# The first DFT stage of batch 1 on quarters of the array: two half-loads, four tied matmuls, two stores a step

## The chip, the core and the metric

The kernel runs on one core of a Trainium2 chip. The metric is the device time of one execution in microseconds (us); several executions are timed and the median counts. One further execution was recorded by the hardware profiler, and all rows shown here come from that one.

## What is computed

The program chains three layers. The change lies in the first, which transforms a tensor of 4 batches, 3072 positions and 256 channels along the positions, applies a complex weight matrix with soft thresholding to the spectrum, and transforms back:

```python
X = np.fft.rfft(x, axis=1)
Yr = Xr @ w_r - Xi @ w_i + b_r
Yi = Xr @ w_i + Xi @ w_r + b_i
Yr, Yi = soft_threshold(Yr, 0.01), soft_threshold(Yi, 0.01)
y = np.fft.irfft(Yr + 1j * Yi, n=3072, axis=1)
```

The second layer sends each token to one of 8 experts (up to 384 tokens each, in order of position), and the third is a feed-forward layer with a gate. Since the experts fill up early, batch 0 and the first third of batch 1 are usually all that is needed; batches 2 and 3 stand in a branch (`far`) that is not taken with these inputs.

## The kernel before

The transform of 3072 points is split into 48 times 64. For batch 1 the **first stage** is `s1`: a 48-point transform over positions that lie 64 apart. Its input is laid out as 96 rows (48 positions, times 2 interleaved halves of the 64), and its table `c1` is a 96 x 96 matrix that holds the 48 x 48 table twice, spread by an identity of size 2, so half of its entries are zero. `s1` walks over 8 pieces of 1024 columns. For each piece, SyncE's queue (SP) loads `xt` (96 rows of 4 KB), TensorE (PE) makes two float32 matmuls of 96 x 96 by 512 columns into one PSUM bank each (pool `ps`, 3 banks), ScalarE (ACT) or VectorE (DVE) copies each bank to `ao`, and SP stores `ao` to `a_d` in DRAM. The profile calls the two `ps<-xt,c`, L406, and a float32 matmul shows as two records, since it is made in two passes.

Around it runs the **spectral stage of batch 0**, `kphase`, in steps over pairs of frequencies: four transposes into `at` (L430, from the same pool `ps`), four float32 matmuls into `xp` (L438), 24 short matmuls into `yp` (L207 to L209), two float32 matmuls into `bp` (L489); ACT and DVE cut and threshold in between, and ACT stores `b_d`. A third stream, `ffn_in`, fetches and reshapes weights of the last layer (`nt`, 512 KB each, and `mixed`). A fourth loads the tables `c2` and `c3` piece by piece (`c<-in_tab`, `c<-in_inv`). `mix` draws steps from these generators in proportion to given lengths, and a scheduler then sets each engine's instruction order when the program is built; on the chip each engine's order is fixed, and so is the order of DMAs on SP's queue.

`self.after(ins, first)` asks only that one instruction stands behind another in that order. After this stretch comes `is2`, the inverse stage of batch 0, which already works on quarters of the array through `tiled` (L363): 48 rows of input on partitions 0 to 47, 48 on 64 to 111, and outputs on PSUM partitions 0 to 63 and 64 to 127.

Of the kernel before, what the change touches and what calls it, by code (L numbers as in the profile page):

```python
# [9 lines left out]
F32 = mybir.dt.float32  # L10
# [6 lines left out]
B, S, D = 4, 3072, 256  # L17
N1, N2 = 48, 64
NK = 24
Q = 96  # L20
TW = 32
E, F, CAP = 8, 1024, 384
DFF = 2048
P = 128
# [25 lines left out]
def _tables():  # L50

    n = float(S)
    t1 = np.arange(N1)
    t2 = np.arange(N2)
    c1 = np.zeros((N1, NK, 2))  # L60
    c4 = np.zeros((NK, 2, N1))
    alt = np.where(t1 % 2 == 0, 1.0, -1.0)
    c1[:, 0, 0] = 1.0
    c1[:, 0, 1] = alt
    c4[0, 0] = 1.0 / n
    c4[0, 1] = alt / n
    for k in range(1, NK):
        a = 2 * np.pi * ((k * t1) % N1) / N1
        c1[:, k, 0] = np.cos(a)
        c1[:, k, 1] = -np.sin(a)  # L70
        c4[k, 0] = 2 * np.cos(a) / n
        c4[k, 1] = -2 * np.sin(a) / n
    eye2 = np.eye(2)
    c1 = np.einsum("akr,pz->apkrz", c1, eye2).reshape(Q, Q)
    third = np.einsum("kra,pz->krpaz", c4[:, :, :QB // 2], np.eye(2)).reshape(Q, QB)

    def halves(t):
        t = np.pad(t.reshape(N1, N1), ((0, 64 - N1), (0, 64 - N1)))
        return np.concatenate([t, t])

    c4 = np.concatenate([halves(c4), np.pad(third, ((0, P - Q), (0, 0)))], axis=1)
    m = np.zeros((NK, 2, N2, 2, N2))
    s = np.arange(N2)
    for k in range(1, NK):
        f = k + N1 * s
        a = 2 * np.pi * ((t2[:, None] * f[None]) % S) / S
        sg = np.where(f > S // 2, -1.0, 1.0)[None]
        co, si = np.cos(a), np.sin(a)
        m[k, 0, :, 0], m[k, 1, :, 0] = co, si
        m[k, 0, :, 1], m[k, 1, :, 1] = -si * sg, co * sg  # L90
    alt2 = np.where(t2 % 2 == 0, 1.0, -1.0)
    inv0 = np.zeros((2, N2, 2, N2))
    for half, f0 in ((0, 0), (1, N1 // 2)):
        for j in range(32):
            f = f0 + N1 * j
            if f == 0:
                continue
            a = 2 * np.pi * ((t2 * f) % S) / S
            sl = 32 * half + j
            m[0, half, :, 0, sl] = np.cos(a)  # L100
            m[0, half, :, 1, sl] = -np.sin(a)
            inv0[0, sl, half] = 2 * np.cos(a)
            inv0[1, sl, half] = -2 * np.sin(a)
    prime = np.concatenate([-m[0, :, :, 1], m[0, :, :, 0]], axis=2).reshape(P, P)
    m[0, 0, :, 0, 0] = 1.0
    m[0, 0, :, 1, 0] = alt2
    inv0[0, 0, 0] = 1.0
    inv0[1, 0, 0] = alt2
    m = m.reshape(NK, P, P)
    tab = np.concatenate([prime, m[0], m[1:].transpose(1, 0, 2).reshape(P, -1)], axis=1)  # L110
    inv = np.concatenate([inv0.reshape(P, P), m[1:].transpose(2, 0, 1).reshape(P, -1)], axis=1)
    ind = np.zeros((2, 2, P))
    ind[:, 0, :64] = 1.0
    ind[:, 1, 64:] = 1.0
    ind[0, 0, 64] = 1.0
    ind[0, 1, 64] = 0.0
    ind = ind.transpose(1, 0, 2).reshape(2, 2 * P)
    u, q = np.arange(P) // QB, np.arange(P) % QB
    at = TW * q + GT * u
    tri = (at[:, None] < at[None]).astype(np.float32)  # L120
    tok = 1 + at[:, None] + (TW * QB * np.arange(3)[:, None] + np.arange(GT)).reshape(1, -1)
    out = {
        "c1": c1,
        "c4": c4,
        "tab": tab,
        "inv": inv,
        "ind": ind,
        "rt": np.concatenate([tri, np.ones((P, P)), tok], axis=1),
    }
    return {k: np.ascontiguousarray(v, np.float32) for k, v in out.items()}  # L130
# [24 lines left out]
class Kernel:  # L155
    def __init__(self, ctx, tc, i, o):
        self.tc, self.nc, self.i, self.o = tc, tc.nc, i, o
        nc = self.nc
        cst = ctx.enter_context(tc.tile_pool(name="cst", bufs=1))
        self.dr = ctx.enter_context(tc.tile_pool(name="dr", bufs=1, space=bass.MemoryType.DRAM))  # L160
        self.zt = cst.tile([P, 1, D], F32, name="zt")
        nc.vector.memset(self.zt, 0.0)
        self.ident = cst.tile([P, P], F32, name="ident")
        make_identity(nc, self.ident)
        self.table = cst.tile([P, NF, SC * E], F32, name="table")
        self.carry = cst.tile([P, E], F32, name="carry")
        nc.gpsimd.memset(self.carry, 0.0)
        nc.gpsimd.memset(self.table, 0.0)
        self.attn = [self.dr.tile([n, D], F32, name=f"attn{h}") for h, n in enumerate((NEAR, NT - NEAR))]
        self.cst = cst  # L170
        self.tail = cst.tile([P, SC, 2, D], F32, name="tail")
        self.mixed = self.dr.tile([DFF // D, P, 3, P], F32, name="mixed")
        self.zeroed = 0
        self.stored, self.fetched, self.spread = {}, None, None
        self.again, self.away, self.evicted, self.gated = False, False, None, {}
        self.held, self.lasty = {}, None

# [41 lines left out]
    @contextmanager  # L219
    def consts(self, tag):  # L220

        with self.tc.tile_pool(name=f"bc{tag}", bufs=2, side="right") as bc:
            self.bc = bc
            self.c1 = bc.tile([Q, Q], F32, name="c1", bufs=1)
            self.nc.sync.dma_start(out=self.c1, in_=self.i["c1"])
            yield

    @contextmanager
# [23 lines left out]
    def near(self):  # L252

        ads, self.bds, self.res = {}, {}, {}
        self.left = ExitStack()
        self.kp = self.left.enter_context(self.tc.tile_pool(name="kpa", bufs=2, reuse_waits="tile"))
        with self.stream("a", 3, "right"), self.sums("a", 2):
            self.warm()
            self.first()
            tables, spectra = self.load_tables(), self.kphase(0, ads)  # L260
            for g in (tables, spectra, tables, spectra, spectra):
                next(g)
            mix([tables, spectra, self.s1(1, ads), self.ffn_in(0, 6, 0)], [4, 10, 24, 7], lead=[0, 0, 0, 0])
            rest = self.kphase(1, ads, True)
            next(rest)
            with self.tc.issue_after(self.fetched):
                self.route_consts()
            mix([self.is2(0, (0, 1, 2), self.res), self.ffn_in(6, 8, 5)], [10, 7])
            self.route(0, (0, 1, 2), self.res)
            self.rank()  # L270
            self.early = self.slots(self.cst, 0, EARLY, self.sel, "s")[0]
            for _ in rest:
                pass
# [80 lines left out]
    CH = 512  # L354
    LD = 1024

    def tiled(self, table, rows, pool):

        out = [pool.tile([P, self.CH], F32, tag="ps", name="ps1") for _ in range(2)]
        for ch in range(2):  # L360
            for p in range(2):
                at = slice(64 * p, 64 * p + N1)
                self.nc.tensor.matmul(out[p][64 * ch:64 * ch + 64], table[at, :64], rows[at, ch * self.CH:(ch + 1) * self.CH],  # L363
                                      start=True, stop=True)
        return out

    def first(self):
# [23 lines left out]

    def s1(self, b, ads):
        nc, bp, ps, CH, LD = self.nc, self.bp, self.ps, self.CH, self.LD
        xv = self.i["x"].rearrange("b (q t) c -> b q (t c)", t=TW)
        a_d = ads[b] = self.dr.tile([NK, P, D], F32, name=f"a_d{b}")
        av = a_d.rearrange("k (r t) c -> (k r) (t c)", r=4)
        for n in range(TW * D // CH):
            half = slice(n * CH % LD, n * CH % LD + CH)
            if half.start == 0:
                ld = slice(n * CH, n * CH + LD)  # L400
                xt = bp.tile([Q, LD], F32, tag="xt", name="xt", bufs=self.sb)
                ao = bp.tile([Q, LD], F32, tag="ao", name="ao1", bufs=self.sb)
                ins = nc.sync.dma_start(out=xt, in_=xv[b, :, ld])
                self.after(ins.ins, self.fetched)
            pt = ps.tile([Q, CH], F32, tag="ps", name="ps1")
            nc.tensor.matmul(pt, self.c1, xt[:, half], start=True, stop=True)  # L406
            self.hi("aava"[n % 4], ao[:, half], pt)
            if half.stop == LD:
                self.stored.setdefault(b, []).append(nc.sync.dma_start(out=av[:, ld], in_=ao).ins)
            yield  # L410

    def kphase(self, b, ads, ahead=False):
# [938 lines left out]
```

## Time and profile before

| | us |
|---|---|
| median of 3 runs (616.84 to 617.54) | 617.31 |
| the profiled execution | 615.97 |
| its span, first to last instruction | 614.2 |
| PE busy in the span | 593.2 (97%) |
| DVE busy | 420.4 (68%) |
| ACT busy | 338.7 (55%) |
| GpSimd (POOL) busy | 196.8 (32%) |

The profiled execution lies 1.3 us under the median of the timed runs, and 1.8 us of it lie outside the span. The mean granted clock of TensorE is 0.993 of its full 2.4 GHz. 86.09 MB were moved by DMA. An engine's busy time is that of its records; PE's records overlap, so the distance from one start to the next tells what a matmul costs, and not its length.

### The profile page before, as it was taken

To read this page: it belongs to the slowest core of one execution; us is meant where nothing else is said; L and a number is where in the kernel's file an instruction comes from. 1 tells how busy PE (TensorE), PEld (TensorE's weight loads), DVE (VectorE), ACT (ScalarE), POOL (GpSimd) and SP (SyncE) were. 2 spreads that over 40 slices of the span, in tenths; PEclk is the share of its full clock that TensorE was granted. 3 is DMA by queue.
4 is the path that set the end of the run, shared out by engine and by line. 5 is a ranking of instruction groups with operands and counts; after the bars stand their busy time and mean duration, and the time that the engine had idled before them with its cause. 6 is when DMAs were issued, how large, how long until landed. Compare 5 with 4: busy or idle time off the path is not lost. (4 is left out here: it accounts for less than half of the span.)

```text
span 614.2 us, 11459 instructions
## 1 busy us (share of the span) xinstructions
PE 593.2 (97%) x4116; PEld 553.2 (90%) x4116; DVE 420.4 (68%) x838; ACT 338.7 (55%) x722; POOL 196.8 (32%) x195
## 2 busy tenths in 40 slices
PE   9999999998999799989999999999999999999993
PEld 9887899666988578979999999999999999999993
DVE  2477775358977579999876785586587677476562
ACT  2646554345535464567755666665567556375561
POOL 1001010001056243267563505435403442163433
PEclk9999999999999999999999999999999999999998
DMA  8838775984456989211734543404533230010001
GB/s 225 253 94 272 251 227 166 246 268 123 162 179 208 259 272 295 92 52 44 222 118 133 154 125 103 153 17 138 153 106 112 85 105 22 5 66 27 16 2 56
DMA packets 65755, 86.09 MB, mean 140 GB/s; under 512 B 5812, under 2 KB 55608, under 8 KB 65688
## 3 DMA queue, kind: packets, MB, share of 16 engines
q1 hardware_dynamic: 53720, 69.53, 37.7%
q10 hardware_dynamic: 9664, 9.44, 5.2%
q0 software_dynamic: 2304, 6.29, 3.2%
q8 instruction: 34, 0.56, 0.4%
q14 instruction: 33, 0.27, 0.1%
HBM read 54.31 MB, written 30.93 MB: 139 GB/s over the span
## 5 line engine op out<-in xcount | busy, mean ns | idle before, releaser
L1249 DVE TENSOR_TENSOR u<-h,u 128x384 f32<-128x384 f32 x224 | 117.8, 552 | 57.2 <-PE h L209 48.3
L1172 ACT ACTIVATE u<-u 128x384 f32<-128x384 f32 x128 | 64.1, 522 | 69.4 <-DVE u L1249 68.8
L208 PE MATMUL o<-wo,gl 128*128 128x256 f32 x366 | 97.9, 280 | 1.5 <-DVE gl L199 1.5
L209 PE MATMUL o<-wo,gh 128*128 128x256 f32 x366 | 98.0, 280 | 0.0
L207 PE MATMUL o<-wo,gh 128*128 128x256 f32 x366 | 86.2, 280 | 0.1
L199 POOL TENSOR_TENSOR ring<-mt,ring 128x384 fp32r<-128x384 f32 x32 | 38.3, 1199 | 128.6 <-ACT ring L191 117.7
L199 POOL TENSOR_TENSOR gl<-u,gh 128x384 fp32r<-128x384 f32 x62 | 65.2, 1068 | 31.6 <-ACT gh L191 27.2
L208 PEld LDWEIGHTS o<-wo,gl 128*128 128x128 f32 x366 | 68.8, 188 | 1.8 <-DVE gl L199 1.8
L209 PEld LDWEIGHTS o<-wo,gh 128*128 128x128 f32 x366 | 68.8, 188 | 0.0
L191 ACT CAST gh<-u 128x384 fp32r<-128x384 f32 x126 | 63.3, 510 | 4.8 <-PE o L209 3.1
L207 PEld LDWEIGHTS o<-wo,gh 128*128 128x128 f32 x366 | 64.4, 188 | 0.4 <-ACT gh L191 0.4
L207 PE MATMUL yp<-wri,xk 128*128 128x256 f32 x188 | 56.2, 299 | 0.0
L1094 DVE SCALAR_TENSOR_TENSOR hl<-hp,hh 128x384 fp32r<-128x384 f32 x64 | 35.2, 552 | 28.6 <-ACT hh L1093 24.8
L209 PE MATMUL yp<-wri,xk 128*128 128x256 f32 x188 | 54.0, 287 | 0.0
L208 PE MATMUL yp<-wri,xk 128*128 128x256 f32 x188 | 53.6, 285 | 0.2 <-issue 0.2
L191 ACT CAST w<-st 128x512 fp32r<-128x512 f32 x64 | 38.7, 619 | 25.2 <-DMA st<-in_moe_w 17.6
L1093 ACT ACTIVATE hh<-hp 128x384 fp32r<-128x384 f32 x64 | 31.0, 490 | 36.7 <-PE y L208 17.3
L199 DVE TENSOR_TENSOR w<-st,w 128x512 fp32r<-128x512 f32 x53 | 38.4, 734 | 18.5 <-ACT w L191 14.0
L199 POOL TENSOR_TENSOR wi<-na,wi 128x256 fp32r<-128x256 f32 (+1 forms) x8 | 8.1, 1011 | 127.7 <-ACT wi L191 127.7
L207 PE MATMUL y<-hh,w 128*128 128x384 f32 x128 | 43.5, 341 | 1.8 <-ACT w L191 1.8
L207 PE MATMUL hp<-xT,w 128*128 128x384 f32 x128 | 43.4, 340 | 1.4 <-ACT w L191 0.7
L208 PE MATMUL y<-hh,w 128*128 128x384 f32 x128 | 43.3, 338 | 0.0
(248 smaller groups left out, 1529.2 us busy)
## 6 DMA issues: line engine op xcount, KB each, us to landing
st<-in_moe_w SPq DMA_DIRECT2D x64, 256.0 KB, 3.0
out<-zt SPq DMA_DIRECT2D x48, 256.0 KB, 2.9
b_d<-bo ACTq DMA_DIRECT2D x12, 512.0 KB, 3.0
mt<-mixed SPq DMA_DIRECT2D x32, 192.0 KB, 2.4
xt<-in_x SPq DMA_DIRECT2D x15, 384.0 KB, 6.3
nt<-in_moe_w_in SPq DMA_DIRECT2D x8, 512.0 KB
nt<-in_moe_w_out SPq DMA_DIRECT2D x16, 256.0 KB, 8.1
a_d<-ao SPq DMA_DIRECT2D x8, 384.0 KB, 3.0
```

The costliest lines, as they stand in the source:

```text
L191: self.lastact = self.nc.scalar.copy(dst, src)
L199: return e.tensor_tensor(dst, src, raw(hi), ALU.subtract).ins
L207: first = nc.tensor.matmul(out, lh, rh, start=start, stop=False)
L208: nc.tensor.matmul(out, ll, rh, start=False, stop=False)
L209: return first.ins, nc.tensor.matmul(out, lh, rl, start=False, stop=stop).ins
L1093: self.rectified = nc.scalar.activation(hh, hp, AF.Relu).ins
L1094: self.evicted = nc.vector.scalar_tensor_tensor(hl, hp, 0.0, raw(hh), ALU.max, ALU.subtract).ins
L1172: act.activation(sg, sg, AF.Silu)
L1249: v.tensor_tensor(to, h, u, ALU.add)
```

## The change

The 48-point table is now also kept in its small form, padded to 64 x 64 on both partition halves (`c1h`), beside the old one, which the first stage of batch 0 still uses; the constant load grows from 96 x 96 to 128 x 160 values. In `s1` a piece's input comes as two loads of 48 rows, to partitions 0 to 47 and 64 to 111. The two matmuls of 96 x 96 by 512 become four of 48 x 64 by 512 by way of `tiled`, in the order upper rows, lower rows, upper, lower, each set behind the one before it by `after`. Each of the two banks now holds 128 x 512 and is copied as before (three of four by ACT). The result leaves in two stores of 48 partitions with rows of 2 KB, in place of one with rows of 4 KB. `s1` has 8 steps where it had 16, and its length in `mix` goes from 24 to 12.

```diff
+    small = c1.copy()
     c1 = np.einsum("akr,pz->apkrz", c1, eye2).reshape(Q, Q)
...
+    wide = np.pad(c1, ((0, P - Q), (0, 0)))
+    c1 = np.concatenate([wide, halves(small)], axis=1)
...
-            self.c1 = bc.tile([Q, Q], F32, name="c1", bufs=1)
-            self.nc.sync.dma_start(out=self.c1, in_=self.i["c1"])
+            c1 = bc.tile([P, Q + 64], F32, name="c1", bufs=1)
+            self.nc.sync.dma_start(out=c1, in_=self.i["c1"])
+            self.c1, self.c1h = c1[:Q, :Q], c1[:, Q:]
...
-            mix([tables, spectra, self.s1(1, ads), self.ffn_in(0, 6, 0)], [4, 10, 24, 7], lead=[0, 0, 0, 0])
+            mix([tables, spectra, self.s1(1, ads), self.ffn_in(0, 6, 0)], [4, 10, 12, 7], lead=[0, 0, 0, 0])
...
-    def tiled(self, table, rows, pool):
+    def tiled(self, table, rows, pool, order=(0, 1)):
 
         out = [pool.tile([P, self.CH], F32, tag="ps", name="ps1") for _ in range(2)]
+        ins = None
         for ch in range(2):
-            for p in range(2):
+            for p in order:
                 at = slice(64 * p, 64 * p + N1)
-                self.nc.tensor.matmul(out[p][64 * ch:64 * ch + 64], table[at, :64], rows[at, ch * self.CH:(ch + 1) * self.CH],
-                                      start=True, stop=True)
+                prev, ins = ins, self.nc.tensor.matmul(out[p][64 * ch:64 * ch + 64], table[at, :64], rows[at, ch * self.CH:(ch + 1) * self.CH],
+                                                       start=True, stop=True).ins
+                if prev and order[0]:
+                    self.after(ins, prev)
...
-        xv = self.i["x"].rearrange("b (q t) c -> b q (t c)", t=TW)
+        xv = self.i["x"].rearrange("b (a p t) c -> b p a (t c)", p=2, t=TW)
         a_d = ads[b] = self.dr.tile([NK, P, D], F32, name=f"a_d{b}")
-        av = a_d.rearrange("k (r t) c -> (k r) (t c)", r=4)
-        for n in range(TW * D // CH):
...
+        av = a_d.rearrange("k (r z t) c -> (k r) z (t c)", r=2, z=2)
+        for n in range(TW * D // LD):
+            xt = bp.tile([P, LD], F32, tag="xt", name="xt", bufs=self.sb)
+            ao = bp.tile([P, 2, CH], F32, tag="ao", name="ao1", bufs=self.sb)
+            for p in range(2):
+                ins = nc.sync.dma_start(out=xt[64 * p:64 * p + N1], in_=xv[b, p, :, n * LD:(n + 1) * LD])
                 self.after(ins.ins, self.fetched)
...
+            for p, pt in enumerate(self.tiled(self.c1h, xt, ps, (1, 0))):
+                self.hi("aava"[2 * n % 4 + p], ao[:, p], pt)
+            for ch in range(2):
+                nc.sync.dma_start(out=av[:, :, n * LD + ch * CH:][:, :, :CH], in_=ao[64 * ch:64 * ch + N1])
             yield
```

The instruction order of PE, ACT, DVE and SP differs between the two programs only from the first matmul of `s1` (37.54 us in the profile before) to about 84 us, apart from the branch that is not taken, the constant load at the start, and the first loads of `xt` that are now pairs. From there on the four engines have the same rows in the same order. Three places follow.

The first place is PE's order where `s1` begins, right behind the first `bp` pair; `ps` is a PSUM bank, `c_78` the table `c1`. Before:

```order
L489 MATMUL bp<-cl,c_226 128x256 x2
L406 MATMUL ps_432<-xt,c_78 96x512
L406 MATMUL ps_446<-xt,c_78 96x512
L438 MATMUL xp<-c_225,ar 128x128 x4
L207 MATMUL yp<-wri,xk 128x256
L208 MATMUL yp<-wri,xk 128x256
L406 MATMUL ps_453<-xt,c_78 96x512
```

The same place of the changed program, where `tiled` is L368:

```order
L493 MATMUL bp<-cl,c_226 128x256 x2
L368 MATMUL ps_434<-xt,c_78 64x512
L368 MATMUL ps_433<-xt,c_78 64x512
L368 MATMUL ps_434<-xt,c_78 64x512
L368 MATMUL ps_433<-xt,c_78 64x512
L442 MATMUL xp<-c_225,ar 128x128 x4
L368 MATMUL ps_459<-xt,c_78 64x512
```

Step 0 stands in one piece, and behind `xp` comes a single matmul of step 1. Sixteen short matmuls into `yp` follow it, and then the rest of step 1:

```order
L210 MATMUL yp<-wri,xk 128x256
L368 MATMUL ps_458<-xt,c_78 64x512
L368 MATMUL ps_459<-xt,c_78 64x512
L368 MATMUL ps_458<-xt,c_78 64x512
L434 MATMUL at<-ident,xs 128x128 x4
```

Step 1 is cut in 1 and 3. Steps 2 to 5 stand in one piece each; the first matmul of step 7 stands right behind the four of step 6, and the other three come ten `yp` matmuls later. So 9 pieces of quarter matmuls stand between other work, where before the 16 matmuls of full size stood.

The second place is SP's queue, from the store of step 0 on (`a_d`; the table pieces are `in_tab` and `in_inv`). Before:

```order
L409 DMA a_d_428<-ao_430 96x1024
L307 DMA c_225<-in_tab 128x768
L307 DMA c_226<-in_inv 128x768
L403 DMA xt<-in_x 96x1024
L409 DMA a_d_428<-ao_451 96x1024
L871 DMA nt<-in_moe_w_in 128x1024
L919 DMA mixed<-mt 128x2x384
L403 DMA xt<-in_x 96x1024
```

In the changed program, from the same store to the second load of `xt` behind it:

```order
L413 DMA a_d_428<-ao_430 96x1x512 x2
L413 DMA a_d_428<-ao_455 96x1x512 x2
L311 DMA c_225<-in_tab 128x768
L311 DMA c_226<-in_inv 128x768
L408 DMA xt<-in_x 48x1024 x2
L875 DMA nt<-in_moe_w_in 128x1024
L413 DMA a_d_428<-ao_539 96x1x512 x2
L923 DMA mixed<-mt 128x2x384
L408 DMA xt<-in_x 48x1024 x2
```

The two tables, and with them step 3's load, stood behind the store of step 0 and stand now behind the store of step 1 (`ao_455`) as well; the store of step 2 (`ao_539`) stands now ahead of step 4's load, the last row of both pieces.

## Rows read from the trace of the kernel before

**Rows 1.** The page: PE's busy time, and PE's busy tenths in 40 slices of 15.4 us.

```profile
PE 593.2 (97%) x4116; PEld 553.2 (90%) x4116; DVE 420.4 (68%) x838; ACT 338.7 (55%) x722; POOL 196.8 (32%) x195
...
PE   9999999998999799989999999999999999999993
```

**Rows 2.** Windows from 37 us: length, busy us (records) by engine, PEclk, DMA share, GB/s.

```profile
37.00:60.00 23.00, 23.00 (x141) 18.08 (x140) 18.01 (x32) 13.50 (x28) 3.48 (x4) 1.00 0.74 227
60.00:82.00 22.00, 22.00 (x140) 17.58 (x138) 16.24 (x28) 13.13 (x28) 3.60 (x4) 1.00 0.81 265
82.00:110.00 28.00, 28.00 (x219) 27.09 (x218) 17.03 (x30) 12.95 (x29) 1.28 (x1) 1.00 0.61 183
110.00:135.00 25.00, 25.00 (x203) 15.47 (x202) 10.03 (x26) 10.26 (x20) 0.00 (x0) 1.00 1.03 269
```

**Rows 3.** Timeline of PE where `s1` begins: start us, us, engine, line, operation, tiles, shapes.

```profile
36.68 1.03 PE L489 MATMUL bp<-cl,c 128*128 128x256 f32 x4
37.54 1.88 PE L406 MATMUL ps<-xt,c 96*96 96x512 f32 x4
39.26 1.06 PE L438 MATMUL xp<-c,ar 128*128 128x128 f32 x8
40.07 0.36 PE L207 MATMUL yp<-wri,xk 128*128 128x256 f32 x1
40.27 0.28 PE L208 MATMUL yp<-wri,xk 128*128 128x256 f32 x1
...
41.97 0.60 PE L430 MATMUL at<-ident,xs 128*128 128x128 f32 x4
42.32 0.36 PE L209 MATMUL yp<-wri,xk 128*128 128x256 f32 x1
42.52 0.28 PE L207 MATMUL yp<-wri,xk 128*128 128x256 f32 x1
42.64 0.28 PE L208 MATMUL yp<-wri,xk 128*128 128x256 f32 x1
```

**Rows 4.** Timeline of PE in `is2`, which works on quarters (L363).

```profile
110.60 1.08 PE L363 MATMUL ps<-br,c 48*64 48x512 f32 x4
111.61 1.13 PE L489 MATMUL bp<-cl,c 128*128 128x256 f32 x4
112.67 1.09 PE L363 MATMUL ps<-br,c 48*64 48x512 f32 x8
113.69 0.39 PE L207 MATMUL yp<-wri,xk 128*128 128x256 f32 x1
113.91 0.28 PE L208 MATMUL yp<-wri,xk 128*128 128x256 f32 x1
```

**Rows 5.** Lines of ACT and DVE, 37 to 85 us: PSUM copies; busy us, mean ns.

```profile
L191 ACT COPY ao<-ps 96x512 f32<-96x512 f32 x12 | 6.9, 583 | 3.8 <-PE ps L406 1.8 <-DMA xt<-in_x 1.1 <-ACT bo L191 0.5
...
L193 DVE COPY ao<-ps 96x512 f32<-96x512 f32 x4 | 2.7, 680 | 0.4 <-PE ps L406 0.4
```

**Rows 6.** Timeline of SP's queue: issue time, issue us; store, table, step 3's, step 4's load.

```profile
40.28 0.33 SPq L409 DMA_DIRECT2D a_d<-ao  x1
40.66 0.42 SPq L307 DMA_DIRECT2D c<-in_tab  x1
...
41.94 0.45 SPq L403 DMA_DIRECT2D xt<-in_x  x1
...
51.16 0.42 SPq L403 DMA_DIRECT2D xt<-in_x  x1
```

**Rows 7.** Window 41 to 55 us; last columns PEclk, DMA share, GB/s.

```profile
41.00:55.00 14.00, 14.00 (x86) 10.88 (x86) 11.16 (x20) 7.98 (x17) 2.74 (x3) 1.00 0.92 282
```

**Rows 8.** Source view of the loads of `xt` in `s1` (L403).

```profile
DMA to landing us min/median/max: 5.5/6.3/7.6
```

**Rows 9.** Windows around the one fall of TensorE's granted clock; columns as in group 2.

```profile
205.00:212.80 7.80, 5.32 (x27) 4.21 (x26) 2.78 (x6) 3.29 (x7) 1.97 (x2) 1.00 1.08 274
212.80:216.20 3.40, 3.40 (x13) 1.30 (x14) 3.37 (x6) 1.63 (x3) 1.84 (x2) 0.50 1.07 258
```

More of the change, by code (lines that the diff above doesn't have):

```diff
@@ L173, in __init__ @@
         self.zeroed = 0
-        self.stored, self.fetched, self.spread = {}, None, None
+        self.fetched, self.spread = None, None
         self.again, self.away, self.evicted, self.gated = False, False, None, {}
@@ L393, in s1 @@
         nc, bp, ps, CH, LD = self.nc, self.bp, self.ps, self.CH, self.LD
-        xv = self.i["x"].rearrange("b (q t) c -> b q (t c)", t=TW)
+        xv = self.i["x"].rearrange("b (a p t) c -> b p a (t c)", p=2, t=TW)
         a_d = ads[b] = self.dr.tile([NK, P, D], F32, name=f"a_d{b}")
-        av = a_d.rearrange("k (r t) c -> (k r) (t c)", r=4)
-        for n in range(TW * D // CH):
[L398 to L403, printed above, removed]
-                self.after(ins.ins, self.fetched)
[L405 to L409, printed above, removed]
+        av = a_d.rearrange("k (r z t) c -> (k r) z (t c)", r=2, z=2)
[4 more added lines that the diff above has]
+                ins = nc.sync.dma_start(out=xt[64 * p:64 * p + N1], in_=xv[b, p, :, n * LD:(n + 1) * LD])
+                self.after(ins.ins, self.fetched)
+            for p, pt in enumerate(self.tiled(self.c1h, xt, ps, (1, 0))):
+                self.hi("aava"[2 * n % 4 + p], ao[:, p], pt)
+            for ch in range(2):
+                nc.sync.dma_start(out=av[:, :, n * LD + ch * CH:][:, :, :CH], in_=ao[64 * ch:64 * ch + N1])
             yield
```

## The prediction

> **What bounds the kernel now.** I read the page first: PE is busy for 97% of the span, in nearly every slice [rows 1]. That share is a mean, so I looked at the stretch that the change touches. In the windows from 37 to 135 us PE's busy time equals the window's length in all four, at the full granted clock, while DVE and ACT are busy for 13 to 18 us of each 22 to 28, and 10 of the last 25 [rows 2]. So in this stretch PE's own instruction order is the bound: what it has less to do there ends everything behind it earlier, and what it waits there is lost in full. The DMA share is the other thing to see: 0.74 and 0.81 in the two windows of `s1`, and within them 0.92 at 282 GB/s from 41 to 55 us [rows 2, 7]. The queues are nearly full just where the change moves them.
>
> **PE's work.** Durations are read from start to start. Four records of L406 (two matmuls) begin at 37.54, and the next group begins at 39.26: 0.86 us for a matmul, 13.76 for the 16 [rows 3]. The other groups have the spacings 0.86 us (`bp` pair, 36.68 to 37.54), 0.89 (`xp`, 39.26 to 40.15, which is the second `yp` matmul at 40.27 less one spacing of 0.12), 0.43 (`at`, 41.97 to 42.40 by the same reckoning) and 0.12 for a `yp` matmul (42.52 to 42.64) [rows 3].
>
> What a piece of quarter matmuls costs I take from `is2`, where the same form runs. Eight records (four matmuls) take from 112.67 to 113.69, 1.02 us; four records (two matmuls) take from 110.60 to 111.61, 1.01 [rows 4]. The price is thus one for a piece, whether it has two matmuls or four on different quarters. Going in and out costs extra: the `bp` pair ahead of the piece lasts 1.06 us (111.61 to 112.67) where 0.86 is usual, so 0.20 for one way out and one way in [rows 3, 4]; the second `yp` matmul behind a piece comes 0.22 after the first, 0.10 more than usual [rows 4]. I take 1.02 + 0.10 + 0.09 = 1.21 us for a piece. The Trainium skill, TensorEngine Tiling (Array Packing), Theoretical Speedup, gives up to a factor of two for each small dimension; by it a step of four quarter matmuls would take the time of one full matmul, 0.86 us, and 6.9 us would be saved. The Trainium skill, under the same title, Key Properties, says that a change of tiling mode drains the engine. The rows above have both: 1.02 in place of 0.86, and about 0.2 for the ways in and out.
>
> Now the nine pieces. Steps 0, 2, 3, 4 and 5 stand alone: 5 x 1.21 = 6.05. Step 1 is cut in 1 and 3: 2 x 1.21 = 2.42. That is more than the 1.72 it cost before. Step 6 has step 7's first matmul behind it. That one uses a quarter that step 6 has just used, so it must wait for it; no row shows this. Its cost lies between nothing and a full matmul, 0.86; four matmuls on different quarters leave no idle quarter in which it could hide, so I take the upper end: 2.07. Step 7's other three cost 1.21. Sum: 6.05 + 2.42 + 2.07 + 1.21 = 11.75, against 13.76: **2.0 us less**. Bounds: 2.9 if the fifth matmul is free; and each way in or out may be off by the whole 0.10, which the other work around it could hide or double, some 0.9 over nine pieces: 1.1 to 3.8.
>
> **ACT, DVE and PSUM.** The 16 copies stay 16, twelve by ACT at 583 ns and four by DVE at 680 [rows 5]. They have 128 partitions instead of 96 and the same 512 elements on each. I price this at nothing, hidden by the idle 9.5 and 8.9 us that ACT has in the two windows (DVE 5.0 and 5.8) [rows 2]. Without that cover it would be the copies of step 0 that hold PE, since a step now takes two of the three banks at once; the order puts 16 `yp` matmuls (1.9 us) ahead of the next matmul that needs a bank again, and two copies take 1.2.
>
> **DMA.** There are 8 loads and 8 stores more, with the same bytes. An issue takes SP 0.3 to 0.45 us [rows 6], some 6 us in a stretch of 45 in which SP mostly waits: nothing by itself. The price lies in what is queued behind what. Before, the two tables and step 3's load were issued from 40.66 on, behind step 0's store [rows 6]. Now they also stand behind step 1's store, and step 1 ends late, since it was cut: step 0 37.54 to 38.75, `xp` 39.64, the single 40.85, sixteen `yp` 42.77, the other three 43.98, their copies about 44.7. So the stream starts some 4.4 us later, at about 45.1, while PE wants the loads earlier. When does PE want them? To step 3 it has four pieces (4.84), three `xp` (2.67), 54 `yp` (6.48), two `at` (0.86) and two `bp` pairs (1.72): 37.54 + 16.57 = 54.1. To step 4 come step 3 (1.21), `at` (0.43), 22 `yp` (2.64), a `bp` pair (0.86) and a quarter of an `xp` (0.22): 59.5.
>
> The seventh `xp` group, which reads the moved table piece, comes at 52.5, 7 us behind its issue. Step 3's load is issued at about 46.8 (its second half, which the first matmul reads). Landing took 5.5 to 7.6 us for these loads [rows 8]: 52.3 to 54.4 against 54.1. Step 4's load has ahead of it, from step 1's store on, two stores of 384 KB, two table pieces of 384, step 3's load of 384, a weight piece of 512, ACT's `b_d` of 512 and `mixed` of 384; with itself 3,712 KB, or 3.80 MB. At 282 GB/s [rows 7] that is 13.5 us, so 45.1 (less the issue, plus the first bytes' way, which I set equal) gives 58.6, and the slowest part lands somewhat later: 58.6 to 60.5 against 59.5. Before, the load was issued at 51.16 [rows 6] and PE came to it at about 59.6, so there was room. I charge 0.4 us of waiting on PE, between nothing (all in time) and 1.0. Waits at the two loads do not add: the first delays PE and so eases the second.
>
> **The constant load** grows from 36 to 80 KB. At 282 GB/s the 45,000 bytes take 0.16 us; the loads of batch 0 stand behind it, and batch 0's first stage may or may not hide that. I take 0.1, between 0 and 0.16.
>
> **Sum.** 2.0 - 0.4 - 0.1 = 1.5 us less. The profiled execution, 615.97 us with 1.8 outside the span, would come to 614.5. The timed median lies 1.3 above it; the same difference on it gives **615.8 us**. A difference of less than 0.2% (1.2 us) can hardly be told from none by a measurement of this kernel.
>
> **Does the gain reach the end?** Behind 84 us all engines have the same rows, and PE is full to 135 us [rows 2]. Later PE does wait, mainly from 205 to 212.8 us, where it is busy for 5.32 of 7.80 us, and the clock then stands at 0.50 (1.2 GHz) for 3.4 us, back at 2.4 GHz behind it [rows 9]. The DMAs on which it waits there are issued behind the routing, and so shift along. What I can't tell is whether the same fall comes again once these gaps have moved: without it up to 1.7 us more are gained, with a second one as much is lost.
>
> **The rivals.**
> - *The late loads eat the gain.* The same rows as above, less kindly: at 228 GB/s step 4's load lands at 61.8, and PE waits 2.3 us. Waits from 0.7 to 3.1 us leave a change of -1.2 to +1.2 us, 616.1 to 618.5. For it: the window's share of 0.92 leaves no spare [rows 7]. Against it: before, the queue had the same bytes to bring and never held PE [rows 2].
> - *Slower: SP's queue behind the cut step 1.* The same place, but with step 4's load landing over 3.1 us behind PE's need, later than 62.6; this outweighs 2.0 less 0.1 by over 1.2. It takes a rate below 217 GB/s over those 3.80 MB. The mean of the whole window 37 to 60, idle start included, was 227 [rows 2], so it is not excluded; at 200 GB/s the load lands at 64.1, PE waits 4.6 us, and the time is 620.0.
> - *The quarters run in turn*, so that a step does not do what it is made for: 4 x 0.86 + 0.19 = 3.63 us in place of 1.72, 15 us in all, 632.6. Against it stand the eight records in 1.02 us [rows 4].
> - *The ways in and out cost nothing and the quarters overlap fully*: 0.86 a step, 6.9 us less, 610.4. Against it: the 1.06 us of the `bp` pair and the 1.02 of the eight records [rows 4]. This is what the speed-up table of the Trainium skill, TensorEngine Tiling (Array Packing), Theoretical Speedup, would give; the trace does not agree, with its 1.02.
>
> **How the numbers follow.** My forecast, a gain of 1.2 to 3.1 us that reaches the end, has 0.56, and its own range is 614.2 to 616.1. The late loads have 0.33, the slower queue 0.07, quarters in turn 0.02, free quarters 0.02. Faster: 0.56 + 0.02 = 0.58. Same: 0.33. Slower: 0.07 + 0.02 = 0.09. The range takes the forecast's own, at the low end a little of the lost fall of the clock, and the late loads up to +0.5 us: 614.0 to 617.8.
>
> **What would show it.** Right, if L368 stands in nine pieces whose next group begins about 1.0 us after their start; if PE has no idle time, or some tenths of a us before steps 3 or 4 that end with the landing of `xt`; and if the first quarter matmul of `is2`, at 110.60 before, begins 1.5 us earlier. Wrong, if PE waits over a microsecond on `xt`, on the table that the seventh `xp` group reads, or on a bank; if a lone matmul on one quarter costs more than the 1.21 of a piece; or if the lead at 110 us is there and gone by the end.

## The result and the profile after

The changed kernel is slower: 624.17 us in the median (623.50 to 624.91) against 617.31 (616.84 to 617.54) for the kernel before in the same session; all ratios here go by fast runs alone, which leaves out a fourth run of the kernel before, 626.76 us. The ratio on record is 1.0128 with a 95% interval of 1.0099 to 1.0157; the two medians alone give 1.011. Measured a second time (after_again below) it was 1.0095 (1.0057 to 1.0132). The prediction was 615.8 us with a range from 614.0 to 617.8 and 9 in 100 for slower. The profiled execution took 624.51 us, with a span of 622.7 us, 8.5 more than before.

PE's busy time and its slices in the page, and the granted clock below them, answer to [rows 1]:

```profile
PE 596.8 (96%) x4148; PEld 554.8 (89%) x4148; DVE 418.9 (67%) x838; ACT 339.3 (54%) x722; POOL 197.5 (32%) x195
...
PE   9999989998999889999999999999999999999994
...
PEclk9999979999999979999999999999999999999998
```

PE is busy for 3.6 us more, although it has less to do: matmuls that run while the clock is down last longer. The windows of [rows 2], one more at the place of the low clock (81.4), and two around the later fall, which answer to [rows 9]:

```profile
37.00:60.00 23.00, 21.49 (x156) 16.27 (x155) 15.66 (x30) 12.75 (x27) 3.01 (x3) 1.00 0.62 183
60.00:82.00 22.00, 18.58 (x135) 14.04 (x136) 14.65 (x26) 10.13 (x22) 2.74 (x3) 0.99 0.79 240
82.00:110.00 28.00, 28.00 (x194) 25.73 (x189) 17.23 (x31) 13.03 (x30) 2.73 (x3) 0.89 0.61 186
110.00:135.00 25.00, 25.00 (x192) 16.96 (x192) 10.52 (x24) 9.66 (x20) 0.00 (x0) 1.00 0.89 240
81.40:88.20 6.80, 6.60 (x26) 4.87 (x27) 2.88 (x5) 3.48 (x9) 1.45 (x2) 0.50 0.60 171
...
217.00:221.40 4.40, 1.87 (x10) 1.23 (x8) 0.51 (x2) 1.44 (x3) 0.80 (x1) 1.00 1.09 283
221.40:228.20 6.80, 6.56 (x23) 4.45 (x24) 5.75 (x9) 3.50 (x7) 3.03 (x3) 0.50 0.87 234
```

PE now lacks 1.5 us in the first window and 3.4 in the second, and then runs 6.8 us at 0.50 (1.2 GHz), which costs 3.4 us more. The DMA share fell from 0.74 to 0.62 in the first window. Cut finer, the window shows that the queues start late and are then as full as the prediction reckoned. Before:

```profile
41.00:47.00 6.00, 6.00 (x36) 4.58 (x36) 3.80 (x8) 3.10 (x7) 1.44 (x2) 1.00 0.91 264
```

After:

```profile
41.00:47.00 6.00, 6.00 (x41) 4.39 (x40) 3.02 (x6) 2.98 (x7) 1.44 (x2) 1.00 0.30 77
47.00:57.00 10.00, 8.49 (x68) 7.07 (x69) 6.59 (x13) 5.01 (x10) 1.56 (x1) 1.00 0.96 283
```

The view of waits says what PE stood at, from 37 to 95 us; in the same view of before there is no row at all:

```profile
PE ps L368 <- ACT ao L194: 3.1, 1, 3.1
PE ps L368 <- DMA xt<-in_x: 1.9, 2, 1.5
```

The waits stand in PE's timeline behind the piece that they hold; the first rows, the start of `s1`, answer to [rows 3]:

```profile
38.45 1.09 PE L368 MATMUL ps<-xt,c 48*64 48x512 f32 x8
39.47 1.16 PE L442 MATMUL xp<-c,ar 128*128 128x128 f32 x8
...
56.48 1.21 PE L368 MATMUL ps<-xt,c 48*64 48x512 f32 x8 [1.51 <-DMA xt<-in_x]
...
74.23 2.03 PE L368 MATMUL ps<-xt,c 48*64 48x512 f32 x10
76.19 1.16 PE L442 MATMUL xp<-c,ar 128*128 128x128 f32 x8
...
81.60 1.98 PE L368 MATMUL ps<-xt,c 48*64 48x512 f32 x6 [3.07 <-ACT ao L194]
```

A step takes 1.02 us, as predicted. The longest wait is that of the last three matmuls of step 7 for a bank that ACT has not copied. ACT's timeline ahead of that moment:

```profile
74.76 0.41 ACT L461 ACTIVATE xk<-xk 128x256 fp32r<-128x256 f32 x1
79.32 0.68 ACT L881 ACTIVATE na<-nt 128x512 f32<-128x512 f32 x1 [4.15 <-DMA nt<-in_moe_w_in]
79.91 0.56 ACT L194 COPY bo<-bp 128x512 f32<-128x512 f32 x1
80.50 0.37 ACTq L496 DMA_DIRECT2D b_d<-bo  x1
80.96 1.07 ACT L194 COPY ao<-ps 128x512 f32<-128x512 f32 x2 [0.49 <-ACT bo L194]
```

ACT is not busy: it stands 4.15 us at the fifth `nt`, a weight load for another layer, and step 6's copies stand behind that in its order. In the kernel before ACT had the same order, with these rows:

```profile
74.11 0.68 ACT L877 ACTIVATE na<-nt 128x512 f32<-128x512 f32 x1 [2.45 <-DMA nt<-in_moe_w_in]
...
75.77 1.07 ACT L191 COPY ao<-ps 96x512 f32<-96x512 f32 x2 [0.49 <-ACT bo L191]
```

PE wanted the next bank at 77.72, for the transposes into `at`, which come from the same pool of three; the last matmul of `s1` came later:

```profile
73.17 2.74 PE L406 MATMUL ps<-xt,c 96*96 96x512 f32 x6
77.72 0.60 PE L430 MATMUL at<-ident,xs 128*128 128x128 f32 x4
80.81 1.02 PE L406 MATMUL ps<-xt,c 96*96 96x512 f32 x2
```

The three matmuls at 73.17 fill the three banks. DVE copies the third of them, and is not done with it at 77.72:

```profile
77.23 0.68 DVE L193 COPY ao<-ps 96x512 f32<-96x512 f32 x1
```

So `at` stands in a bank that ACT copied, and the first of these was free at 76.35 (75.77 and a copy of 0.58 us): the room was 1.4 us. From the first `bp` pair (36.68 before, 37.49 after) the copies now start 4.4 us later (39.09, then 43.47), and a bank is wanted at the same time as before (77.72 - 36.68 = 41.04; 81.60 - 3.07 - 37.49 = 41.04). 4.4 less 1.4 is 3.0, and the wait is 3.07. That PE does not want the bank earlier, though it has less to do, is owed to the 1.9 us it has waited at `xt`: where these waits are gone (st_act and st_pool below), it wants a bank at 38.7.

Why is `nt` late? SP's timeline (it answers to [rows 6]):

```profile
40.71 6.06 SPq L413 DMA_DIRECT2D a_d<-ao  x4
46.81 1.65 SPq L311 DMA_DIRECT2D c<-in_tab  x1
...
49.05 1.41 SPq L408 DMA_DIRECT2D xt<-in_x  x2
...
72.85 1.20 SPq L413 DMA_DIRECT2D a_d<-ao  x2
74.09 0.67 SPq L875 DMA_DIRECT2D nt<-in_moe_w_in  x1
```

The table that was issued at 40.66 goes out at 46.81, step 3's load at 49.05 in place of 41.94, and the fifth `nt` at 74.09, right behind step 5's stores. There it stood before, too:

```profile
68.91 0.31 SPq L409 DMA_DIRECT2D a_d<-ao  x1
69.31 0.38 SPq L871 DMA_DIRECT2D nt<-in_moe_w_in  x1
```

Counted from the first `bp` pair, step 5's store goes out 3.1 us later (32.23, then 35.36), `nt` follows it after 1.24 us in place of 0.40, and ACT begins on it 5.23 us behind its issue in place of 4.80: together the 4.4 us. The store is late because DVE's copy for it is, and that copy stands behind DVE's own operation on the fourth `nt`, for which DVE waited:

```profile
68.91 0.43 DVE L886 TENSOR_SCALAR nsg<-nt 128x512 int32<-128x512 int32 x1 [2.55 <-DMA nt<-in_moe_w_in]
72.10 0.68 DVE L196 COPY ao<-ps 128x512 f32<-128x512 f32 x1
```

The source view adds how long SP is occupied by the issue of a store, the middle one of the three times being the median in ns. Before:

```profile
L409 SPq DMA_DIRECT2D a_d<-ao x8: 310/324/331, 40.3 to 82.5; - x8
```

After:

```profile
L413 SPq DMA_DIRECT2D a_d<-ao x16: 547/584/1895, 40.7 to 85.5; - x16
```

The accounting from the first `bp` pair to the first quarter matmul of `is2`: 73.92 us before, 80.12 after (117.61 - 37.49). Taking off the waits (4.94) and what the clock costs (3.40) leaves 71.78: the matmuls are 2.1 us cheaper, as predicted. To the 6.2 us of this stretch come 0.8 us by which all stood later ahead of `s1`, and 1.7 us from the second fall, 6.8 us long where it was 3.4; that makes 8.7 us where the span grew by 8.5, so 0.2 came back elsewhere.

### The profile page after: what moved, and what is told of

Same layout as the page of the kernel before. It is cut to its first block, busy times and chain, and to the rows that moved or that the text cites. A ratio compares the mean times of both kernels' runs of the same rounds, so it can differ in the third digit from the quotient of the medians.

```text
span 622.7 us, 11552 instructions
## 1 busy us (share of the span) xinstructions
PE 596.8 (96%) x4148; PEld 554.8 (89%) x4148; DVE 418.9 (67%) x838; ACT 339.3 (54%) x722; POOL 197.5 (32%) x195
## 5 line engine op out<-in xcount | busy, mean ns | idle before, releaser
L194 ACT CAST w<-st 128x512 fp32r<-128x512 f32 x64 | 38.7, 619 | 23.7 <-DMA st<-in_moe_w 15.4
L202 DVE TENSOR_TENSOR w<-st,w 128x512 fp32r<-128x512 f32 x53 | 38.7, 739 | 17.9 <-ACT w L194 14.6
```

What stands on the lines that cost most here:

```text
L194: self.lastact = self.nc.scalar.copy(dst, src)
L202: return e.tensor_tensor(dst, src, raw(hi), ALU.subtract).ins
```

## The experiments

The theory after the result: *SP's queue*. The stores of steps 0 and 1, twice as many and longer to issue, stand ahead of the tables, loads and `nt`; a late `nt` holds ACT and DVE, hence the next copies and stores, and so the next `nt`. Rivals: *banks* (two of three banks for a step hold PE in any case), *halves* (the number of DMAs, wherever they stand), *start* (the larger constant load), and chance.

This table has every run. Its second column is the start of ACT's operation on the fifth `nt`, the fourth the first quarter matmul of `is2`, both counted from the first `bp` pair; the third is the view of PE's waits from 37 to 100 us. The fourth column holds what a fall of the clock costs in the stretch: 3.4 us in the changed kernel, c1_split, st_behind and both, 1.7 in after_again, abs_behind, order2, s7_later and st_act_s7, nothing in the others.

| kernel | `nt` at ACT | PE waits, us | to `is2`, us | ratio to before (95%) |
|---|---|---|---|---|
| before | 37.43 | none | 73.92 | 1 |
| changed | 41.83 | bank 3.1, `xt` 1.9 | 80.12 | 1.0128 (1.0099 to 1.0157) |
| after_again | 41.54 | bank 2.9, `xt` 1.8, `xk` 0.3 | 79.15 | 1.0095 (1.0057 to 1.0132) |
| st_act | 37.41 | bank 0.9 | 72.62 | 0.9981 (0.9952 to 1.0010) |
| st_pool | 37.17 | bank 0.8 | 72.47 | 1.0030 (0.9990 to 1.0071) |
| c1_split | 41.39 | bank 2.9, `xt` 1.7 | 79.56 | 1.0089 (1.0048 to 1.0129) |
| b_ld2 | 40.26 | `xt` 0.6 | 74.70 | 1.0030 (0.9997 to 1.0063) |
| st_behind | 44.10 | `xt` 2.2, bank 2.1 | 79.61 | 1.0091 (1.0057 to 1.0125) |
| abs_behind | 42.51 | `xt` 2.4, `xk` 2.0 | 78.47 | 1.0064 (1.0023 to 1.0104) |
| b_order | 41.07 | `xt` 1.0 | 75.48 | 1.0001 (0.9974 to 1.0028) |
| order2 | 39.84 | bank 2.7, `xt` 0.5, `xk` 0.2 | 77.05 | 1.0068 (1.0043 to 1.0093) |
| s7_later | 42.18 | `bp` 4.8, `xt` 2.0 | 80.48 | 1.0150 (1.0122 to 1.0179) |
| both | 40.83 | `bp` 6.7 | 80.67 | 1.0126 (1.0101 to 1.0151) |
| b_dma2 | 42.34 | `xt` 0.5 | 74.91 | 1.0040 (1.0013 to 1.0068) |
| nt5_pool | 38.36 | `xt` 1.8, `ps` behind ACT's `xk` 1.1, `xk` 0.9 | 76.58 | 1.0118 (1.0074 to 1.0163) |
| st_act_s7 | 37.73 | `ar` 3.3, `xk` 0.4 | 76.57 | 1.0076 (1.0042 to 1.0109) |
| st_pool_s7 | 35.65 | `xk` 0.3 | other order | 0.9982 (0.9958 to 1.0006) |

**Stores off SP's queue** (st_act; st_pool has `gpsimd` in place of `scalar`):

```diff
-                nc.sync.dma_start(out=av[:, :, n * LD + ch * CH:][:, :, :CH], in_=ao[64 * ch:64 * ch + N1])
+                nc.scalar.dma_start(out=av[:, :, n * LD + ch * CH:][:, :, :CH], in_=ao[64 * ch:64 * ch + N1])
```

> The changed kernel with the stores of `ao` issued by ACT's queue, so that SP's queue holds no store of `s1`; PE's order is the same to 84 us but for a few `yp` matmuls. Theory 'SP's queue': the tables, `nt` and the loads of `xt` stood behind stores whose copies were late; they go out several us earlier, ACT and DVE no longer stand at `nt`, the bank for step 7 is free in time. PE's waits of 1.5, 0.4 and 3.1 us before 84 us go, and with the last of them the clock's fall of 6.8 us (worth 3.4): 624.2 - 8.4 = about 616, down to 614 if the later fall shortens too. Rival 'banks': two of three banks for a step hold PE however the DMAs stand; only the 1.9 us at `xt` go, the 3.1 us and the fall stay: about 622. Rival 'ACT': 16 issues of some 0.5 us on ACT make its copies late, PE waits on banks elsewhere: 620 or more.

> The changed kernel with the stores of `ao` issued by POOL's queue; PE's order changes at two places of some four rows. Theory 'SP's queue': as with ACT's queue, about 616 (614 to 617), with ACT free of the issues. Rival 'banks': about 622, the wait of 3 us on the bank of step 7 and the fall behind it stay. Rival 'POOL': a store that waits on POOL for its copy holds the subtractions into `wi` behind it, and these hold the buffers of `nt`: then `nt` is late again and the time is 620 or more.

Both bring the fifth `nt` back to where it was before (37.4 and 37.2 us), both waits at `xt` go, and so does the fall behind the bank wait. What is left in the trace of st_pool, in the view of PE's waits, is one row:

```profile
PE ps L368 <- ACT ao L194: 0.8, 1, 0.8
```

From `bp` to `is2` they are 1.3 and 1.45 us ahead of before. That speaks for the queue, and the 0.8 for a part of the rival *banks*: in both, ACT's copies start 38.9 to 39.0 us after the first `bp` pair, as before, and PE wants a bank at 38.7, 2.3 us earlier than before. ACT's 16 issues did no harm that shows. The times agree for st_act; those of st_pool spread from 612.3 us (clock 0.996) to 621.2 (0.985), so its ratio tells little.

**The constant load** (c1_split): the old table alone first, the small one in a load behind batch 0's inputs.

```diff
...
+            self.c1h = self.bc.tile([P, 64], F32, name="c1h", bufs=1)
+            self.after(nc.sync.dma_start(out=self.c1h, in_=self.i["c1"][:, Q:]).ins, self.loads[-1])
```

> The changed kernel with the old table of 96 x 96 alone loaded first, and the small one in a load of its own behind the inputs of batch 0; no engine's order changes otherwise. Theory: the 0.8 us by which everything stood later ahead of `s1` (first `bp` group 37.49 after 36.68) came from the larger constant load; it goes and all else stays, 623.4. Rival 'the start sets the clock': with the start as before, the fall at 81 us does not come: 620 or less. Rival 'chance': the start differs from run to run whatever the load, 624.2.

All the waits stay, and the time with them. The first `bp` pair is at 36.99; over all runs it lies between 36.61 and 38.03, and at 37.87 in b_ld2 with the old load. So the 0.8 us at the start differ from run to run, and the larger load is not shown to cost anything.

**Halves and order in the kernel before** (b_ld2: two loads; b_dma2: two loads and two stores; b_order: the queue's order of the changed kernel, with the tables set behind step 1's store in the same way):

```diff
-                ins = nc.sync.dma_start(out=xt, in_=xv[b, :, ld])
-                self.after(ins.ins, self.fetched)
+                for p in range(2):
+                    ins = nc.sync.dma_start(out=xt[48 * p:48 * p + 48], in_=xv[b, 48 * p:48 * p + 48, ld])
+                    self.after(ins.ins, self.fetched)
...
+                if n in (6, 8):
+                    self.after(ins.ins, self.stored[b][n // 2 - 2])
```

> The kernel before with each load of `xt` in `s1` as two loads of 48 rows, nothing else changed; PE's order is the same to 84 us but for a few rows. Theory 'SP's queue': the loads alone cost SP some 0.4 us a step, but none of the tables and stores changes its place, so within 0.5 us of before, 617.0 to 618.0. Rival 'more DMAs': the number of loads itself makes `nt` late and PE waits: 619 or more.

> The kernel before, with its full-size matmuls and single DMAs, but with the tables and step 3's load set behind step 1's store, and step 4's load behind step 2's store, as SP's queue stands in the changed kernel. PE's order changes at three places from some 55 us on. Theory 'place in SP's queue' alone: here step 1's copies are ready some 2 us earlier than in the changed kernel, since step 1 is not cut over 16 `yp` matmuls, so the tables and `nt` come 1 to 2 us later than before, not 4; a wait of 1 us or less: ratio 1.000 to 1.004. If the place in the queue is all and the cut and the halves are nothing, the whole loss comes: ratio 1.008 or more.

> The kernel before, with each load of `xt` as two of 48 rows and each store as two of 2 KB rows; full-size matmuls. PE's order to 84 us is the same but for a few rows; in SP's queue one half of step 1's store stands ahead of the tables. Theory 'place in the queue': that half is ready with the first of step 1's copies, at some 42.5 us, so the tables come about 2 us later and all else is as before: PE waits 0 to 1 us, 74 to 75.5 us from the first `bp` group to the inverse stage, ratio 0.999 to 1.003. Rival 'halves': the issues alone make `nt` late and a bank or `xt` holds PE: 77 us or more, ratio 1.006 or more.

Each costs 0.8 to 1.6 us between `bp` and `is2`, and next to nothing to 0.4% in time. But look at their `nt`: it is late by 2.8 to 4.9 us in all three, as in the changed kernel. In b_dma2 ACT comes to it here, behind one of the copies:

```profile
75.63 0.58 ACT L191 COPY ao<-ps 96x512 f32<-96x512 f32 x1 [0.82 <-PE ps L407]
79.73 0.69 ACT L879 ACTIVATE na<-nt 128x512 f32<-128x512 f32 x1 [3.52 <-DMA nt<-in_moe_w_in]
```

and no bank holds PE. The bank copied at 75.63 serves `at` at 79.24, and the one copied behind `nt`, at 80.32, is wanted only by the full-size matmul at 82.21; ACT's order in b_ld2 is the same in this. In b_order both copies stand behind `nt`, the first ends at 79.39, and `at` comes at 79.87, 42.7 us behind the first `bp` pair where it was 41.0: a wait was missed by 0.5 us. A late `nt` alone is therefore not enough; PE must want the bank that ACT holds back before ACT comes to it. Whether the kernel before would wait with its own orders and a `nt` later by 4.4 us was not run; the room of 1.4 us suggests that it would.

**The same on the changed kernel: order.** after_again is the changed kernel itself. st_behind sets the stores of step n behind the loads of step n + 2; order2 does so for steps 1 and 2 only, which gives SP's order of before.

```diff
+                for st in late.get(n - 2, ()) if n < 5 and n > 2 else ():
+                    self.after(st, ins.ins)
```

> The changed kernel as it is, for the comparison on the same chip: 1.2% slower than before as in the first measurement, with PE's waits at `xt` (1.5 and 0.4 us) and at the bank of step 7 (3.1 us) and a fall of the clock right behind the last. If these were chance, they do not come again and the time is within 0.3% of before.

> The changed kernel with all 16 stores still on SP, but those of step n set behind the loads of step n + 2: the tables, step 3's load and then step 4's, 6's and 7's come ahead of stores that wait. PE's order to 84 us is the same but for one place of ten rows, step 1 still cut. Theory 'place in SP's queue': the tables go out behind step 0's store alone, `nt` is on time, the bank wait and the fall go: 8 us less than the changed kernel, ratio to before 0.995 to 1.003. Rival 'number of DMAs': 32 issues of half the size, at 0.55 us for a store, hold SP wherever they stand; the waits stay, ratio 1.008 or more.

> The changed kernel with two pins: step 1's stores stand behind step 3's loads and step 2's behind step 4's. SP's queue then has the order of the kernel before, with the same 16 half-loads and 16 stores as the changed kernel; PE's order is the changed kernel's row for row, and ACT and DVE differ at one place, where the fourth `nt` stands behind a cut of `xk`. Theory 'place in the queue': the tables and the third `nt` go out some 4 us earlier, the waits at `xt` go; `nt` five lands by about 76, the bank wait shrinks to 1 us or goes, no fall at 81 us: from the first `bp` group to the first quarter matmul of the inverse stage 73 to 74 us (80.1 and 79.2 in the changed kernel, 73.9 before), ratio to before 0.996 to 1.002. Rival 'halves': 32 shorter transfers with SP's longer issues keep `nt` late in any order: 77 us or more, ratio 1.006 or more.

after_again has the same waits, so they are not chance. But the theory as I had put it falls here. In both kernels PE comes to step 6 without a wait, so the place of the tables and early loads did cause the waits at steps 3 and 5. The bank wait stays in order2:

```profile
PE ps L368 <- ACT ao L194: 2.7, 1, 2.7
PE ps L368 <- DMA xt<-in_x: 0.5, 1, 0.5
```

st_behind makes new waits of its own: step 7's load and the fifth `nt` now stand behind stores that wait. In order2 the fifth `nt` comes at 39.84, 2.4 later than before. SP's timeline and its own waits from 64 to 72 us divide this:

```profile
64.93 5.97 SPq L409 DMA_DIRECT2D xt<-in_x  x4
71.01 1.19 SPq L415 DMA_DIRECT2D a_d<-ao  x2
72.25 0.83 SPq L877 DMA_DIRECT2D nt<-in_moe_w_in  x1
```

```profile
SPq L409 <- DMA b_d<-bo: 3.6, 1, 3.6
```

Step 5's store goes out 0.75 us later than before, counted from the first `bp` pair; its two halves, 584 ns (median) for a store in order2 too, put `nt` 0.84 us further behind it; and ACT begins on `nt` 0.82 us later behind its issue. So the longer issues are a third. The 0.75 us come from SP, which had stood 3.6 us at the landing of a store of `b_d` ahead of step 7's loads: the last of step 5's copies was done at 70.12. What ties these loads to `b_d` is not shown.

**ACT's order, PE's order, and one DMA.** abs_behind moves ACT's operation on the fifth `nt` behind step 6's copies; s7_later moves step 7's four matmuls behind the next `bp` pair; both is s7_later with order2; nt5_pool issues the fifth `nt` alone from POOL's queue.

```diff
+        if len(self.abss) == 5 and len(self.cps) > 13:
+            self.after(ins, self.cps[13])
...
+                if self.nb == 1:
+                    self.after(self.s7, self.backed)
...
+            self.nts += 1
-            ins = nc.sync.dma_start(out=t[:, dv], in_=sv.bitcast(I32).rearrange("p (n z) -> p n z", z=2))
+            ins = (nc.gpsimd if self.nts == 5 else nc.sync).dma_start(out=t[:, dv], in_=sv.bitcast(I32).rearrange("p (n z) -> p n z", z=2))
```

> The changed kernel with one instruction moved: ACT's first operation on the fifth `nt` (512 elements, at 79 us) stands behind step 6's two copies of banks, where it stood ahead of them. SP's order is the same, so `nt` and `xt` are as late as before. Theory: the bank wait of 3.1 us at 81 us is ACT standing in order at `nt`; it goes (under 0.5 us left) and with it the fall of the clock, while the waits of 1.5 and 0.4 us at `xt` stay: 6 us less than the changed kernel, ratio 1.000 to 1.004. Rival 'the copies themselves are late' (two banks copied by ACT alone): the wait stays and the ratio is 1.010 or more. Rival 'DVE': DVE stands at the same `nt` and PE now waits for its cut of `xk`, 2 us or more at some 80 us: ratio 1.006 or more.

> The changed kernel with the four matmuls of step 7 set behind the next `bp` pair, some 25 `yp` matmuls later in PE's order, where the kernel before has its last full-size matmul; SP's queue is the same as in the changed kernel. Theory 'a late ACT and a step that wants two of three banks at once': `nt` stays late (landing at about 79), ACT's copies of step 6 come late as before, but PE wants the banks only about 4 us later: no wait on a bank at 78 to 84 us, no fall there; the waits of 1.9 us at `xt` stay: 75 to 76.5 us from the first `bp` group to the inverse stage, ratio 1.000 to 1.004. Rival 'displaced': DVE and ACT stand at `nt` and PE waits for a cut of `xk` instead: 78 us or more, ratio 1.006 or more.

> Both edits: the queue's order of the kernel before, and step 7 set behind the next `bp` pair. If both theories hold, neither wait at `xt` nor wait on a bank is left, and the matmuls' gain of 2.0 us stands alone: 72 us from the first `bp` group to the inverse stage (73.9 before), ratio 0.995 to 0.999. If a late `nt` is only passed on, 74 us or more and a ratio of 1.000 or more.

> The changed kernel with one DMA moved: the fifth `nt` is issued by POOL's queue in place of SP's. PE's and DVE's order are the same row for row, SP keeps all else, ACT differs in one swap (its first operation on this `nt` stands behind a copy of `bo`). Theory: in every run the bank for step 7 came free 2.3 to 2.4 us behind the landing of the fifth `nt`, since ACT stands there in order; with that landing at about 70 us (79.2 before the move) the wait of 2.9 to 3.1 us at the bank and the fall of the clock behind it go, and the waits of 1.9 us at `xt` stay: 73.5 to 75.5 us from the first `bp` group to the inverse stage (80.1 and 79.2 in the changed kernel), ratio 1.000 to 1.005. Rival 'passed on': the sixth `nt`, behind the stores of steps 6 and 7, is as late as before and PE waits 2 us or more at 88 to 93 us: 77 us or more, ratio 1.007 or more.

In abs_behind the bank wait is gone, as the theory has it, and a wait of 2.0 us for a cut of `xk` stands at 91.9 in its place, behind the sixth `nt`; the rival had named it at some 80 us. The clock falls behind that one, and the ratio, 1.0064, is the rival's. In s7_later PE stands at `bp` instead:

```profile
80.34 1.13 PE L498 MATMUL bp<-cl,c 128*128 128x256 f32 x4 [1.10 <-ACT bo L195]
93.05 1.32 PE L498 MATMUL bp<-cl,c 128*128 128x256 f32 x4 [3.69 <-ACT bo L195]
```

ACT's copy of `bo` stands behind the fifth `nt` (79.12 there) and later behind the sixth (91.85), so a PE that is held at no `ps` bank is held at the next one; in the run both, the waits at `bp` grow to 6.7 us (its profiled execution took 631.0 us, the other five 622 to 624). When PE wants the banks is not a cure by itself. nt5_pool is the cleanest: ACT comes to `nt` at 76.34 without waiting for it, and the three matmuls of step 7 start at 80.09 without a wait:

```profile
75.89 1.99 PE L369 MATMUL ps<-xt,c 48*64 48x512 f32 x10 [1.11 <-ACT xk L462]
80.09 1.08 PE L369 MATMUL ps<-xt,c 48*64 48x512 f32 x6
```

So the landing of this one load is what held the bank at 81 us. The stretch to `is2` gets 2.6 to 3.5 us shorter, less than the 73.5 to 75.5 expected, since 1.1 us come back at step 6 and 0.9 at `xk` behind the sixth `nt`. In time no gain shows (1.0118, where 1.000 to 1.005 was expected): there are only four runs, and in the profiled one the clock fell at 145.5 for 7 us, where it had not in the changed kernel.

**Both cures** (stores off SP and step 7 later):

> Both cures together: the stores of `ao` on ACT's queue (then `nt` lands as early as before), and step 7's four matmuls behind the next `bp` pair (then two banks are wanted only when ACT has copied step 6). Theory: each alone left a wait (0.9 us at the bank with the stores on ACT; 1.1 and 3.7 us at `bp` with step 7 late and `nt` late); together neither is left, and the 2 us of matmul time come out whole: 71.5 to 72.3 us from the first `bp` group to the inverse stage (73.9 before), ratio 0.994 to 0.998. Rival 'passed on': the wait comes back at `bp`, 73 us or more and a ratio of 0.999 or more.

> The same with the stores of `ao` on POOL's queue in place of ACT's. Theory: as there, 71.3 to 72.3 us from the first `bp` group to the inverse stage and a ratio of 0.994 to 0.998; the 16 issues cost ACT nothing here, so it may be 0.2 us less. Rival: stores that wait on POOL hold the subtractions into `wi`, `nt` is late again at 80 us: 74 us or more, ratio 1.002 or more.

With ACT's queue a new wait appears:

```profile
PE xp L447 <- DMA ar<-a_d: 3.3, 1, 3.3
PE yp L212 <- DVE xk L464: 0.4, 1, 0.4
```

`ar` is the first input of batch 1's spectral stage, read back from `a_d` when the last store has landed, and step 7 later means that store later; the ratio is 1.0076, where 0.994 to 0.998 was expected. With POOL's queue only 0.3 us of waiting are left up to 100 us. Its PE order differs in `is2`, so its stretch is not compared, but the time can be: 0.9982 (0.9958 to 1.0006), the best with st_act, and not safely apart from the kernel before. Against the changed kernel, the ratios of these two are some 1% lower.

## Why the prediction was wrong

*The matmuls* were right: 1.02 us a step and 2.1 us less (2.0 predicted). The lone first matmul of step 7 cost a piece more, as charged: 1.96 us from 74.23 to 76.19 for the five, priced at 2.07. "Free quarters" and "quarters in turn" are out.

*The step that failed* is "ACT, DVE and PSUM": "I price this at nothing, hidden by the idle 9.5 and 8.9 us that ACT has". That idle time was no room. In the trace before ACT waited 2.45 us for the fifth `nt` with step 6's copies behind it in its order, and PE needed their bank 1.4 us after the first of them. The prediction looked at the banks of step 0 alone. The right check was the time between that copy and that need, against what the change does to either end: `nt` became 4.4 us later, and the need, which would have come some 2 us earlier, was put back by the waits at `xt`. The copies themselves stayed as they were, 586 ns against 583 [rows 5], as the changed kernel's groups of lines from 37 to 85 us show:

```profile
L194 ACT COPY ao<-ps 128x512 f32<-128x512 f32 x12 | 6.6, 586 | 3.4 <-PE ps L368 2.9 <-ACT bo L194 0.5
```

The Trainium skill, TensorEngine Tiling (Array Packing), Gotcha 1: PSUM Pressure, says that different row tiles write to different banks and so raise the pressure on PSUM; the trace agrees in that a step fills two of the three banks, and the wait that is left when the copies are not late is 0.9 us (st_act). The 3.07 us are not owed to that pressure alone, since before, too, `at` wanted a bank at that time.

*The DMA step* had the right place and followed the wrong loads. "An issue takes SP 0.3 to 0.45 us" was 0.58 for the stores and 0.65 for the half loads (median of ten from 37 to 90 us, 0.42 for the five loads before, and 0.37 for the half loads of st_act, where the stores have left this queue). With this, step 3's load was issued at 49.05, where the prediction has 46.8 and the later start of the stretch would make it 47.6; the queue's rate, 283 GB/s, was as reckoned. The waits at `xt` were 1.9 us where 0.4 (0 to 1.0) was charged; step 4's load, on which the rival "slower" hung, held nothing, and step 3's and step 5's did. I left `nt` out, although the order showed it behind the same stores, because PE doesn't read it. It is read by ACT and DVE, which PE needs.

*The clock.* Its fall was foreseen only around 212 us; the one at 81 us, 6.8 us at 0.50, made a wait of 3 us into a loss of 6.5.

What stays open: how the lateness of `nt` divides, over the whole chain of stores, between the longer issues, the order and the halves; at its last link it is divided above. Taken alone in the kernel before, half loads, order, and half loads with half stores make it 2.8, 3.6 and 4.9 us late, so the parts do not add up. And the ratios follow the stretch up to `is2` only roughly, since falls of the clock behind it differ from trace to trace.

## What to carry to other kernels

Idle time of an engine that works in order is room only if what it waits for can't become later: look up what its idle time waits for, and what stands behind. When a change makes an engine on the critical path faster or moves DMAs, list for each buffer that this engine waits for the time between release and need, and follow all loads in the moved queue, those of other layers too, to the engines that read them.

## What was not expected of the hardware

- The store with two runs of 2 KB on each of 48 partitions took 584 ns to issue on SP (596 on ACT, 579 on POOL), and the one with one run of 2 KB on each of 96 partitions in b_dma2 310; both have 96 runs. The store of the kernel before, one run of 4 KB on each of 96 partitions, took 324. So it is the form and not the run's length that makes the issue longer here.
- Behind the wait of 3.07 us the clock stood at 0.50 for 6.8 us; behind the wait of 1.51 at 56 us it did not fall. In after_again, with a wait of 2.89, it stood low from 81 to 85 only.
- Executions of one kernel on one chip lay up to 9 us apart, with the mean clock: st_pool had 612.3 us at 0.996 and 621.2 at 0.985.
